# One attention and feed-forward program on one core: value windows loaded on 128 partitions, and its line of 2036 steps written anew

## The chip, the cores and the metric

The program runs on one core of one Trainium2 chip. The core has a matrix engine (PE, with its weight loads PEld), VectorE (DVE), ScalarE (ACT), GpSimd (POOL), and SyncE (SP), which here only issues DMAs. GpSimd issues DMAs too, those that add to what lies in DRAM. The metric is the device time of one execution in microseconds, lower is better. It was measured three times: 592.06 us is the median, 590.71 and 593.77 the ends.

## What is computed

Attention with a sliding window of 16 and with 24 block summaries of keys and values, then two feed-forward layers, the first with a softplus, all in fp32 accuracy:

```python
B, H, S, D = 2, 8, 768, 64;  block, window, nb = 32, 16, 24
k_sum = k.reshape(B, H, nb, block, D).max(axis=3)
v_sum = v.reshape(B, H, nb, block, D).mean(axis=3)
scores_l = where(|i - j| < window, q @ k.T / 8, -1e9)
scores_s = q @ k_sum.T / 8 + log(block)
a = softmax(concat([scores_l, scores_s]))
attn = a @ concat([v, v_sum])              # -> x: 1536 x 512
h = x @ w_in;  g = softplus(h);  x2 = g @ w_out      # 512 -> 2048 -> 512
out = ((x2 @ w1) * (x2 @ w2)) @ w3 @ w_out2          # 512 -> 1024 -> 1024 -> 512
```

## The kernel before

**Tiling.** The 12 query tiles (two batches of six) hold 128 positions each, as two blocks of 64. A block sees a window of W = 96 keys and values and the NBK = 24 summaries of its batch, together NK = 120 rows. For a tile t the steps are: `q{t}` and `vw{t}` load its queries and its two value windows; `kw{t}` and `ks{t}` copy its keys and key maxima together; `A{t}` is the score matmul; `max{t}{e}` on DVE and `exp{t}{e}` on ACT are the softmax in eight pieces; `inv`, `norm` scale; `T{t}{h}` transposes on PE, `at{t}{h}` copies that out of PSUM; `AV{t}` multiplies by the values; `xh{t}` and `xl{t}` split the result in a high and a low part, since each fp32 product is made of three passes over such parts (function `mm3`).

**Values.** `vw_load` (L372) issues one DMA for a tile: 96 partitions, on each two rows of 512 floats (2 KB), the two windows of the tile; 384 KB. The summaries come into rows 96 to 119 later: `vss{t}` sums the windows on PE, `vsT` copies the sums, and for tiles 0 and 1 they reach the value tile over PE and a copy (`vsu0`, `vs0_0`, `vs0_1`, `vs1_0`, `vs1_1`), for the others over DRAM (`vsd`, then `vs{t}`). Keys are loaded by `kp0_0` to `kp1_1` (four parts of 384 KB, batch 0) and `kl2`, `kl3` (768 KB each, batch 1); `km2`, `km3` reduce the latter on DVE.

**Feed-forward.** Weights arrive as raw fp32 (`lw...`, three raw slots called st), are made into parts by four conversions (`ca`, `cb`, `cc`, `cd`) and two splits (`ce`, `c`), on ACT, DVE and POOL. `H`, `X`, `Ph` are PE steps of the first layer (plain and, for four pairs, a seven-product scheme with sums `R`, `T` and copies `u1`, `U2`, `U3`), `sa`, `sb`, `sc`, `hi`, `lo` its softplus and split. A finished group of four goes out by `Xo` (a copy) and `Xs` (a DMA that writes, or from GpSimd one that adds to the rows in DRAM); `Xl` loads the sums back. `wm` multiplies w3 by the last weight matrix, ahead of time; `AB`, `Pp`, `O` are the second layer; `Oo` copies the output out of PSUM and `Os` stores it.

**Order.** Nothing is scheduled when it is built: the string `LINE` (L79) names all 2036 steps in the order in which they are issued, with `@` the buffer slots that a step takes and with `:A`, `:D`, `:G` the engine (ACT, DVE, POOL) where a step has a choice. `Order.order` checks that every step stands behind what it needs. Each engine works its own instructions strictly in that order and waits where an input or a slot isn't ready. The times in the code (`COST`, `PACE`, `lead`, `tail`) take no part in what is built.

```python
nc.sync.dma_start(vw[t][0:W], bass.AP(
    tensor=src.tensor, offset=src.offset, ap=[[D, W], [(w1_ - w0) * D, 2], [1, D]]))
```

Of the kernel before, what the change touches and what calls it, by code (L numbers as in the profile page):

```python
# [83 lines left out]
max16 exp25 max17 vss3 exp17 inv2 exp16 norm20:D exp15 T00@0 norm21:D inv1 T01@1 km2 at00:A@1 norm10:G vss6@1 norm11:G T10@0 vss4 at10:A@2 vss5
at01:A@3 T21@0 vsT0 km3 vsd0 vsu0@3 at21:A@4 T20@1 vs0_1:A T11@0 vs0_0:D vs1_1:A vss7 ccw_in0:D@0 at11:A@5 AV0@0 caw_in0:D cbw_in0 cdw_in0 xh0:A@1
vw8@0 vs1_0:D cew_in0:A@0 lw_in1@0 A3@1,2 xl0 caw_in3:A cw_in0:G at20:D@0 A4@0,3 q9@0 max30@0 vs5 kw6:G@2 max31 exp30 vs2 max32 AV1@0 exp31 q6@1 max33
exp32 kw7:G@0 vs3 max34 exp33 max35 vs4 max36 exp35 vw11@3 vss8 max37 exp36 max40@2 A5@1,2 exp37 max41 exp34 max42 max43 xh1:A inv3 kw8:G@1 q7@2 exp41
norm30:D exp40 exp42 norm31:G exp43 max44 ccw_in1:A@1 T30@0 xl1 exp44 max45 ks7 exp45 max46 AV2@0 max47 exp46 at30:D@1 exp47 ks6 ks8 inv4 max50@1
norm41:G max51 exp50 T31@1 exp51 vw9@2 xh2:D A6@0,3 norm40:G at31:A@3 xl2 max52 AV3@0 kw9:G@2 q8@1 max53 exp52 max54 exp53 max55 exp54 max56 T40@0
exp55 vw10@1 max57 ks9 exp56 T41@1 caw_in1:D exp57 cbw_in1 A7@1,2 at40:A@2 inv5 at41:A@5 cdw_in1 vss9 xh3:A norm50:G q10@2 max60@0 cew_in1:A@1  # L90
lw_out3@0 xl3 exp60 max61 cw_in1:G AV4@0 max62 exp61 max63 exp62 max64 exp63 max65 vss10 norm51:G exp64 max66 vss11 exp65 max67 max70@2 T50@0 kw11:G@0
max71 vsT1 exp67 vsd1 max72 T51@1 exp66 at50:D@0 xh4:A@2 A8@0,3 inv6 at51:A@4 max73 norm61:G max74 exp73 vs6 AV5@1 max75 exp74 max80@1 vs7 exp75 max81
vs10 norm60:G xl4 exp70 vs8 T61@0 xh5:A vs9 caw_in2:D kw10:G@1 q11@1 T60@1 at61:A@1 xl5 vs11 at60:A@3 ccw_in2:D@2 exp72 max76 AV6@0 max77 exp76
cbw_in2 exp77 exp71 cdw_in2 H0_0_0@1 exp81 inv7 H0_0_1 cew_in2:A@2 lw_out0@1 max82 norm70:G max83 exp82 A9@1,2 max84 exp83 max85 exp84 norm71:G max86
T70@0 exp85 max87 ks10 exp87 H0_0_2 cw_in2:G exp86 at70:D@2 xh6:A H0_0_3 cbw_in3 exp80 T71@1 He0_0:A@0 A10@0,3 inv8 at71:A@5 xl6 ccw_in3:A@3 norm81:G
H0_1_0@1 max90@0 caw_out0:A max91 AV7@0 norm80:G max92 exp90 max93 exp92 max94 cdw_in3 exp94 T80@0 xh7:A ks11 H0_1_1 max95 lw_out1@2 exp93 xl7
cew_in3:A@3 H0_1_2 max96 exp95 max97 cw_in3:G H0_1_3 at80:D@0 exp96 exp97 max100@2 T81@1 ccw_out3:D@4 He0_1:A A11@1,2 at81:A@4 max101 max102 exp91
max103 AV8@0 exp101 inv9 exp103 max104 caw_out3:D norm90:G exp104 max105 H0_2_0@1 xh8:A@0 max106 max107 exp106 H0_2_1 xl8 norm91:G exp107 H0_2_2
cbw_out3 exp105 exp102 H0_2_3 exp100 max110@1 T90@0 max111 He0_2:A@1 inv10 max112 T91@1 exp111 norm101:G max113 exp112 H0_3_0@0 max114 cdw_out3 exp113
norm100:G exp114 H0_3_1 at91:A@3 max115 H0_3_2 lw_out2@0 cbw_out0 exp115 at90:A@1 H0_3_3 cew_out3:A@2 AV9@0 max116 exp110 cw_out3:D exp116 max117  # L100
He0_3:A ccw_out0:D@0 T100@1 exp117 cdw_out0 T101@0 xh9:A at100:D@2 H1_0_0@1 lw_in4@1 at101:A@5 inv11 H1_0_1 cew_out0:A@3 caw_out1:D norm110:G xl9
caw_out2:A AV10@3 ccw_out2:D@1 spl norm111:G cbw_out1 T110@1 xh10:D H1_0_2 at110:A@0 xl10 H1_0_3 caw_in4:A cw_out0:G cbw_out2 T111@0 He1_0:A@4
H1_1_0@0 at111:A@4 H1_1_1 sa0_0@1 sa0_1@3 sb0_0 AV11@1 cdw_out2 sb0_1 sc0_0 lw_in6@0 cew_out2:A@5 H1_2@1 sc0_1 xh11:A cw_out2:G sa0_2@2 xl11 sb0_2
# [1154 lines left out]
```

## Time and profile before

| | us |
|---|---|
| median of three timed runs (lowest, highest) | 592.06 (590.71, 593.77) |
| the profiled execution | 593.24 |
| its span, first to last instruction | 591.5 |
| PE busy in the span | 551.9 |
| DVE busy | 460.5 |
| ACT busy | 274.9 |
| POOL busy | 170.2 |

The profiled execution is one run; 1.7 us of its time lie outside the span. The granted clock of PE is at its full level over most of the span and at half of it in a few stretches, 0.972 in the mean. The views used below are the page itself, the list of who waits for whom, the chain of waits that ended last, stretches of time with the busy time of each engine, the timeline, and the DMA view. SPq is SyncE issuing DMAs. A number in square brackets in a timeline row is how long the engine sat idle before the row, and what ended that.

### The profile page before, as it was taken

Reading aid. Unit: us, or ns where it says so; the run is one execution under the profiler, and the core shown is the slowest. Engines: PE = TensorE matmul, PEld = TensorE weight load, DVE = VectorE, ACT = ScalarE, POOL = GpSimd, SP = SyncE. Lnnn points to the kernel's source line nnn. Section 1 sums busy time; section 2 is a strip of 40 time slices with the busy share of each in tenths; the row PEclk is TensorE's granted clock in tenths of the full one; section 3 lists DMA queues with packets and bytes.
Section 4 is the critical chain, followed back from the end, with each engine's and each line's share of the span. In section 5 each row is a group of like instructions: output and inputs, shape, how many; then the busy total and the mean of one; then the engine's idle time right before and its main releaser. Section 6 shows DMA issues by size and latency. Waiting matters only on the chain.

```text
span 591.5 us, 8926 instructions
## 1 busy us (share of the span) xinstructions
PE 551.9 (93%) x3228; PEld 449.3 (76%) x3228; DVE 460.5 (78%) x891; ACT 274.9 (46%) x600; POOL 170.2 (29%) x152
## 2 busy tenths in 40 slices
...
GB/s 217 237 299 205 104 76 101 204 148 158 256 173 237 91 156 81 105 165 169 103 108 93 207 272 303 353 135 205 160 127 19 0 73 1 1 1 0 1 32 111
DMA packets 33621, 81.08 MB, mean 137 GB/s; under 512 B 3977, under 2 KB 4425, under 8 KB 33577
## 3 DMA queue, kind: packets, MB, share of 16 engines
...
HBM read 58.91 MB, written 21.59 MB: 136 GB/s over the span
## 4 chain that ended last, share of the span: by engine, by line
PE 48%; DVE 24%; DMA 16%; issue 5%; ACT 4%; POOL 1%; SPq 1%; DVEq 0%; ACTq 0%; POOLq 0%
PE abps L711 17%; PE ops L223 11%; PE abps L223 7%; DMA raw<-in_w_dram 6%; PE wps L223 4%; PE xps L223 3%; DVE cv L266 3%; DVE raw L254 3%; DMA kt<-in_k_dram 3%; PE hps L223 2%; DVE gt L232 2%; DMA qt<-in_q_dram 2%; DVE tm L500 2%; DMA x_d<-xo 2%; DVE cv L262 2%
## 5 line engine op out<-in xcount | busy, mean ns | idle before, releaser
L223 PE MATMUL xps<-gt,w 128*128 128x512 f32 x576 | 136.3, 389 | 0.0
L223 PEld LDWEIGHTS xps<-gt,w 128*128 128x128 f32 x576 | 108.1, 188 | 22.5
L223 PE MATMUL hps<-xt,w 128*128 128x512 f32 x384 | 93.9, 393 | 3.5 <-DVE gt L232 3.5
L232 POOL TENSOR_TENSOR w<-cv,w 128x512 fp32r<-128x512 f32 x34 | 50.7, 1497 | 137.0 <-ACT w L227 89.7
L223 PEld LDWEIGHTS hps<-xt,w 128*128 128x128 f32 x384 | 71.1, 188 | 19.4 <-DVE gt L232 4.8
L223 PE MATMUL ops<-w,pt 128*128 128x512 f32 x288 | 70.3, 389 | 0.0
L254 DVE SCALAR_TENSOR_TENSOR raw<-raw 128x512 int32<-128x512 int32 x72 | 57.0, 796 | 9.5 <-ACT raw L250 9.2
L223 PEld LDWEIGHTS ops<-w,pt 128*128 128x128 f32 x288 | 54.1, 188 | 11.2
L266 DVE SCALAR_TENSOR_TENSOR cv<-cv,raw 128x512 int32<-128x512 int32 x72 | 55.4, 779 | 1.3
L532 POOL DMA_DIRECT2D x_d<-xo x36 | 32.6, 1079 | 79.1 <-ACT xo L227 72.7
L250 ACT ACTIVATE raw<-raw 128x512 int32<-128x512 uint16 x53 | 35.7, 674 | 35.8 <-DMA raw<-in_w_dram 19.4
L723 DVE TENSOR_TENSOR u<-u,abps 128x512 f32<-128x512 f32 x36 | 24.6, 684 | 34.0 <-PE abps L711 20.1
L223 PE MATMUL wps<-w 128*128 128x512 f32 x192 | 47.0, 407 | 3.3 <-DVE w L229 3.3
L503 ACT ACTIVATE tm<-tm 128x512 f32<-128x512 f32 x48 | 29.7, 631 | 41.7 <-DVE tm L500 37.8
L223 PEld LDWEIGHTS wps<-w 128*128 128x128 f32 x192 | 37.9, 198 | 12.1 <-ACT w34o L227 3.7
L227 ACT CAST w<-cv 128x512 fp32r<-128x512 f32 x59 | 35.6, 619 | 22.7 <-DVE cv L266 10.3
L223 PE MATMUL abps<-x2t,w 128*128 128x512 f32 x192 | 44.5, 389 | 0.0
L415 ACT ACTIVATE s<-s,sm 128x120 f32<-128x120 f32 x96 | 36.8, 386 | 10.8 <-DVE sm L409 10.7
L223 PEld LDWEIGHTS abps<-x2t,w 128*128 128x128 f32 x192 | 36.0, 188 | 7.5
L260 ACT ACTIVATE cv<-raw 128x512 f32<-128x512 f32 x48 | 31.7, 671 | 14.9 <-DMA raw<-in_w_dram 7.9
L711 PE MATMUL abps<-t,s 128*128 128x512 f32 x144 | 36.5, 390 | 0.0
L227 ACT COPY u<-abps 128x512 f32<-128x512 f32 x26 | 14.9, 587 | 44.8 <-PE abps L711 33.3
(128 smaller groups left out, 878.9 us busy)
## 6 DMA issues: line engine op xcount, KB each, us to landing
...
```

The lines of the kernel that those rows point to most:

```text
L223: nc.tensor.matmul(ps, lhs(a), rhs(b), start=first and i == 0, stop=last and i == 2)
L227: nc.scalar.copy(d, s_)
L232: EN[eng].tensor_tensor(d, a, b, ALU.subtract)
L250: nc.scalar.activation(r[:, :, 0], r.bitcast(U16)[:, :, 1], AF.Copy, bias=-(0.5 - 2.0 ** -14), scale=2.0 ** -13)
L254: nc.vector.scalar_tensor_tensor(r[:, :, 0], r[:, :, 1], -0x80000000, r[:, :, 0], ALU.bitwise_and, ALU.bitwise_or)
L260: nc.scalar.activation(f(c), h, AF.Copy, scale=2.0 ** -112)
L266: nc.vector.scalar_tensor_tensor(c, c, 3, r[:, :, 0], ALU.logical_shift_left, ALU.bitwise_or)
L415: nc.scalar.activation(s[:, e], s[:, e], AF.Exp, bias=sm[:, 0, e:e + 1], scale=-1.0, accum_out=sm[:, 1, e:e + 1])
L503: nc.scalar.activation(tm[c, i], tm[c, i], AF.Softplus)
L532: nc.gpsimd.dma_start(x2_d[4 * c + o], xo[c, g, o], accum_op=ALU.add)
L711: nc.tensor.matmul(ps, w[:, a, (o + kk) * P:(o + kk + 1) * P], rhs(b), start=k in (1, 5, 2) and kk == 0 and n == 0, stop=kk == 1 and n == ...
L723: nc.vector.tensor_tensor(tu[z, j, d], tu[z, j, d], bank[z, j, k], ALU.add)
```

## The change

Two things change: the value load, and the line.

```diff
@@ vw_load
-                four[0] = xt_p.tile([NK, 4, 2, D], F32, tag=slot("xt"), name="vw4")
+                four[0] = xt_p.tile([P, 4, 2, D], F32, tag=slot("xt"), name="vw4")
...
-            vw[t] = ap_.tile([NK, 2, D], F32, tag=slot("vw"), name="vw")
-        nc.sync.dma_start(vw[t][0:W], bass.AP(
-            tensor=src.tensor, offset=src.offset, ap=[[D, W], [(w1_ - w0) * D, 2], [1, D]]))
+            vw[t] = ap_.tile([P, 2, D], F32, tag=slot("vw"), name="vw")
+        n = P if w1_ + P <= S else W
+        nc.sync.dma_start(vw[t][0:n], bass.AP(
+            tensor=src.tensor, offset=src.offset, ap=[[D, n], [(w1_ - w0) * D, 2], [1, D]]))
@@ att_d1
-                        vw[t][:, blk, 64 * h:64 * h + 64],
+                        vw[t][:NK, blk, 64 * h:64 * h + 64],
@@ LINE, its first and its last row
-sz ml kp0_0@0 z@0 sell1 busy@0 sell0 sell2 kp0_1 kp1_0@1 kp1_1 q0@0 vw0@0 vw3@1 q1@1 vw2@2 kn0_0 q2@2 vw4@0 vw5 vw1@3 vw6 kw0:A@0 kw1:D@1 il kl2@2
...
-O20_0 O21_0 O23_2 O22_0 O23_0 Oo20:D@5 Oo22:A@2 Oo23:D@0 Os20 Os22 Oo10:D@4 Os23 Oo21:D@1 Os10 Os21
...
+Oo20:A@2 O17_3 Os20 O18_3 O23_2 O17_1 O18_1 O19_1 O20_1 O21_1 O22_1 O23_1 O19_3 Oo21:A@3 O20_3 Oo10:A@0 Oo12:D@5 Os21 Oo11:A@4 Os10 O21_3 Oo22:A@1
+Os12 O22_3 Oo13:A@2 Os11 Os22 O23_3 Os13 Oo23:D@3 Os23
```

The load now fills 128 partitions (512 KB) for ten of the tiles; for tiles 5 and 11 the second window ends at the last row of the input, and they stay at 96. Rows 96 to 119 are still overwritten by the summaries, rows 120 to 127 are read by nobody. The line holds the same 2036 steps in another order, with other slots, and 252 of them on another engine; PE has the same 3228 matmuls. Steps other than DMAs on POOL are 104 (99 before), and 76 (70 before) of them stand ahead of the first `AB`; DVE instructions are 896 (891).

Three places, as the built programs have them. A row is a source line (one more after the change), the operation, what is written and read, and its size.

SP at the start of the program; `vw` and `vw4` are value tiles, `kt` keys, `qt` queries, `sel_t` a small constant. Before:

```order
L303 DMA kt_172<-in_k_dram 128x768 x2
L364 DMA qt_175<-in_q_dram 128x512
L381 DMA vw_177<-in_v_dram 96x2x512
L381 DMA vw_179<-in_v_dram 96x2x512
L364 DMA qt_181<-in_q_dram 128x512
L381 DMA vw_183<-in_v_dram 96x2x512
L364 DMA qt_187<-in_q_dram 128x512
L381 DMA vw4_189<-in_v_dram 96x2x512 x2
L381 DMA vw_192<-in_v_dram 96x2x512
L381 DMA vw4_189<-in_v_dram 96x2x512
L897 DMA id_t_127<-in_ident_dram 128x128
L303 DMA kt_202<-in_k_dram 128x1536
```

After:

```order
L303 DMA kt_170<-in_k_dram 128x768 x2
L382 DMA vw_173<-in_v_dram 128x2x512
L332 DMA sel_t_128<-in_sel_dram 64x2
L364 DMA qt_176<-in_q_dram 128x512
L364 DMA qt_178<-in_q_dram 128x512
L382 DMA vw_180<-in_v_dram 128x2x512
L898 DMA id_t_127<-in_ident_dram 128x128
L364 DMA qt_183<-in_q_dram 128x512
L382 DMA vw4_185<-in_v_dram 128x2x512
L382 DMA vw4_185<-in_v_dram 96x2x512
L382 DMA vw4_185<-in_v_dram 128x2x512
L332 DMA sel_t_128<-in_sel_dram 64x2
```

The same loads stand between the fourth key part and the large key loads; all but one are wider, and their order among themselves is another.

ACT in the middle of the first layer; `u_2944` before and `u_2937` after is the copy `U3h5`, `raw_2879` before is the raw weight tile w3 6 (`caw36` works on it), `raw_2769` after is w_out 12. Before:

```order
L227 CAST gt_2913<-hps_2861 128x512
L250 ACTIVATE raw_2874<-raw_2874 128x512
L260 ACTIVATE cv_2923<-raw_2874 128x512
L250 ACTIVATE raw_2879<-raw_2879 128x512
L227 COPY u_2944<-abps_2622 128x512
L227 CAST w_2947<-cv_2882 128x512
```

After:

```order
L260 ACTIVATE cv_2907<-raw_2859 128x512
L227 CAST gt_2911<-u_2713 128x512
L260 ACTIVATE cv_2920<-raw_2769 128x512
L227 COPY u_2937<-abps_2616 128x512
L227 CAST w_2944<-cv_2920 128x512
L504 ACTIVATE tm_2955<-tm_2955 128x512
```

`caw36` is no longer ahead of the copy (it went to DVE); the conversion ahead of it now reads a tile whose load is issued 13 PE steps earlier.

SP where the sums of the first layer are loaded back (`x2f`, steps `Xl0_0` to `Xl0_3`); `raw_3557` before and `raw_3281` after is the raw weight tile w3 8 (step `lw38`). Before:

```order
L539 DMA x2f_3408<-x2_d2_111 128x512
L539 DMA x2f_3400<-x2_d1_110 128x512
L539 DMA x2f_3408<-x2_d3_112 128x512
L273 DMA cv_3459<-pk_wo23_88 128x512
L273 DMA cv_3472<-pk_w35_98 128x512
L273 DMA cv_3477<-pk_wo24_89 128x512
L269 DMA pk_wo27_92<-cv_3497 128x512
L241 DMA raw_3520<-in_w3_dram 128x1024
L273 DMA cv_3527<-pk_wo25_90 128x512
L273 DMA cv_3534<-pk_w36_99 128x512
L269 DMA pk_wo26_91<-cv_3525 128x512
L241 DMA raw_3557<-in_w3_dram 128x1024
```

After:

```order
L241 DMA raw_3198<-in_w3_dram 128x1024
L273 DMA cv_3209<-pk_w30_93 128x512
L241 DMA raw_3226<-in_wo2_dram 128x1024
L273 DMA cv_3271<-pk_w31_94 128x512
L269 DMA pk_wo26_91<-cv_3260 128x512
L241 DMA raw_3281<-in_w3_dram 128x1024
L273 DMA cv_3289<-pk_wo20_85 128x512
L540 DMA x2f_3424<-x2_d0_109 128x512
L540 DMA x2f_3424<-x2_d1_110 128x512
```

The load of w3 8 and the store `pkwo26` (`pk_wo26`) stood behind the loads of the sums and now stand ahead of them.

## Rows read from the trace of the kernel before

**Rows 1.** The page, part 1: busy time of PE, share, instructions.
```profile
PE 551.9 (93%) x3228; PEld 449.3 (76%) x3228; DVE 460.5 (78%) x891; ACT 274.9 (46%) x600; POOL 170.2 (29%) x152
```

**Rows 2.** Stretches: length, busy us (instructions) by engine, PE clock, DMA share, GB/s.
```profile
11.60:37.30 25.70, 15.14 (x256) 11.86 (x256) 14.15 (x69) 12.49 (x54) 6.05 (x9) 0.73 1.05 273
37.30:93.00 55.70, 49.99 (x844) 41.08 (x844) 49.60 (x216) 51.10 (x187) 30.78 (x36) 0.97 0.50 139
...
400.00:585.00 185.00, 184.86 (x816) 152.75 (x814) 131.17 (x196) 53.17 (x90) 41.12 (x29) 1.00 0.15 50
```

**Rows 3.** The chain of waits at 19 to 35 us, at 261 and 351: start, us, what.
```profile
19.26 15.50 DMA kt<-in_k_dram
34.79 1.75 DVE ks L308
...
260.82 9.80 DMA raw<-in_w_dram
...
351.42 17.76 DMA raw<-in_w_dram
```

**Rows 4.** Timeline: the last key part's reduction on DVE, and `AV0` on PE.
```profile
10.26 0.95 DVE L308 TENSOR_REDUCE ks<-kt 128x24 f32<-128x768 f32 x1 [0.99 <-DMA kt<-in_k_dram]
...
37.33 0.86 PE L453 MATMUL av<-at,vw 120*64 120x64 f32 x22 [1.93 <-DVE vw L229]
```

**Rows 5.** DMA view of 10 to 22 us, of 32 to 36, of 586.4 to 589.9.
```profile
DMA packets 1458, 2.75 MB, mean 229 GB/s; under 512 B 124, under 2 KB 124, under 8 KB 1457
...
DMA packets 475, 1.57 MB, mean 393 GB/s; under 512 B 54, under 2 KB 54, under 8 KB 474
...
DMA packets 707, 1.30 MB, mean 373 GB/s; under 512 B 70, under 2 KB 70, under 8 KB 707
```

**Rows 6.** The page, part 5: groups, with busy us and mean ns of one.
```profile
L254 DVE SCALAR_TENSOR_TENSOR raw<-raw 128x512 int32<-128x512 int32 x72 | 57.0, 796 | 9.5 <-ACT raw L250 9.2
...
L415 ACT ACTIVATE s<-s,sm 128x120 f32<-128x120 f32 x96 | 36.8, 386 | 10.8 <-DVE sm L409 10.7
```

**Rows 7.** Timeline: a DVE step held by POOL at 142.
```profile
142.52 1.78 DVE L254 SCALAR_TENSOR_TENSOR raw<-raw 128x512 int32<-128x512 int32 x1
```

**Rows 8.** Timeline around 231 us: `ccwo24` on DVE, `R11` and `cw_in13` on POOL, `Ph2_4`.
```profile
231.34 4.55 DVE L262 TENSOR_SCALAR cv<-raw 128x512 f32<-128x512 f32 x1
...
234.03 1.56 POOL L232 TENSOR_TENSOR w<-cv,w 128x512 fp32r<-128x512 f32 x1
235.81 0.68 DVE L254 SCALAR_TENSOR_TENSOR raw<-raw 128x512 int32<-128x512 int32 x1
...
237.15 2.49 PE L711 MATMUL abps<-xt,w 128*128 128x512 f32 x6 [3.64 <-DVE gt L232]
```

**Rows 9.** Timeline around 271 us: `caw36` and `U3h5` on ACT, `Ph4_5` on PE.
```profile
270.71 0.65 ACT L250 ACTIVATE raw<-raw 128x512 int32<-128x512 uint16 x1 [0.97 <-DMA raw<-in_w_dram]
271.26 0.56 ACT L227 COPY u<-abps 128x512 f32<-128x512 f32 x1
...
271.88 2.50 PE L711 MATMUL abps<-t,w 128*128 128x512 f32 x5 [2.90 <-ACT u L227]
```

**Rows 10.** Timeline: the issue of `lw38` on SP, and `wm8` on PE.
```profile
342.67 0.42 SPq L241 DMA_DIRECT2D raw<-in_w_dram  x1
...
375.01 7.19 PE L223 MATMUL wps<-w 128*128 128x512 f32 x18 [3.27 <-DVE w L229]
```

**Rows 11.** Stretches behind the first and last of those waits, columns as in rows 2.
```profile
237.70:241.10 3.40, 3.40 (x9) 2.67 (x8) 1.12 (x1) 1.43 (x3) 0.67 (x1) 0.50 0.71 236
...
374.20:381.00 6.80, 5.99 (x14) 4.72 (x15) 6.40 (x13) 6.80 (x13) 0.00 (x0) 0.50 1.03 374
```

**Rows 12.** Timeline of the last 12 us: the last `O` steps, `Oo` copies, `Os` stores.
```profile
579.72 5.15 PE L223 MATMUL ops<-w,pt 128*128 128x512 f32 x22
...
584.90 2.48 DVE L229 COPY osb<-ops 128x512 f32<-128x512 f32 x4 [10.27 <-PE ops L223]
585.62 2.41 SPq L746 DMA_DIRECT2D out_dram<-osb  x5
```

More of the change, by code (lines that the diff above doesn't have):

```diff
@@ L84 @@
[L84 to L103, printed above, removed]
@@ L128 @@
-sa0_9@0 ccw35:A@3 lo0_8 sb0_9 X2_5_1 caw35:A sc0_9 R10:G@6 cbw35 hi0_9:A@5 H0_10@1 cew_out11:A@4 ccw_in14:A@4 caw_in14:A cw_out11:G Th1s Ph1_4@1 cdw35
-Th1h:A@0 X2_6_0 sa0_10@3 pkw35 lwo24@1 u1h4:A@0 Th1l sb0_10 X2_6_1 sc0_10 X2_7_0 R21:G@0 hi0_10:D@2 lo0_10 X2_7_1 lo0_9 cawo24:A cbw_in14 H0_11@1 Th3s
-Th2s Th3h:A Ph5_4@0 Th3l Th2h:A@1 Ph1_5@0 Th2l sa0_11@5 Xo21_2:A@4 Ph6_4 Xo21_3:A@1 cdw_in14 Xs21_2 sb0_11 Xo21_0:D@2 Xs21_3 lwo25@2 X0_8_1@0,3
-U2h4:A@1 sc0_11 Xs21_0 u1h5:A@2 ccwo24:D@0 hi0_11:A@1 R11:G@6 cbwo24 Ph6_5 Xo21_1:A@0 lo0_11 cew_in14:A@4 cdwo24 cew_in13:A@1 Ph2_4@1 Ph7_4 cw_in13:G
@@ L136 @@
-pkw32 lw36@0 lo1_9 ccw_out15:A@2 caw_out15:D X1_9_1 Xo02_2:A@0 sa0_12@3 upwo20@3 sa1_10@4 Xs02_2 sb0_12 cbw_out15 X1_8_0@3,0 sb1_10 sc0_12 sc1_10
-hi0_12:A@6 X1_9_0 caw_out12:A lo0_12 ccw_out12:A@4 hi1_10:D@4 cbw_out12 H0_13@0 lo1_10:D caw36:A cdw_out15 U3h5:A@2 cdw_out12 cew_out15:A@0 lw_out13@1
-C22h5 cew_out12:A@3 lw_out14@2 cw_out15:G Ph4_5 cbw36 cw_out12:G Ph3_5 sa1_11@5 sa0_13@1 sb1_11 X1_10_0 C12h5 Shh71:A@2 sb0_13 sc1_11 Slh71:G H0_14@1
-sc0_13 caw_out14:A hi1_11:D@5 hi0_13:D@2 lo1_11 lo0_13 X1_10_1 sa0_14@2 cbw_out14 sb0_14 H0_15@0 ccw36:D@2 upw30@4 sc0_14 upwo21@0 caw_out13:D
@@ L156 @@
-cew37:A@3 cdw38 caw310:A cbw315 cew312:A@5 Xl1_3 lw311@1 cw312:D Xl1_1 wm6 cw37:G ccw310:A@0 cbw310 ccw39:A@4 cdw310 wm3 Xl2_2@3 cdw39 Xl2_0@5 lw20@2
-cew39:A@0 lw10@0 cw39:D wm7 cew38:D@1 wo0:A@0 cw38:D wo1:A@1 ws0 caw311:A ccw311:D@1 ws1 ccw314:A@4 cbw311 Xl2_3 x2h10:A@2 cdw314 wm8@0,1 Xl2_1
-wo3:D@3 wo2:A@2 cdw311 cew314:A@2 ws3 ws2 caw20:A cw314:D lw21@1 cew313:A@0 cbw20 ccw10:A@2 wm9 cw313:D ccw20:A@4 cew310:D@1 caw10:A cdw20 cw310:G
-x2h11:A cbw10 lw11@2 cdw10 cew20:A@1 wm12@0,1 cew311:A@0 x2h21:A@0 cw311:G cw20:D lw12@0 x2l21 wm10 caw21:D ccw21:A@3 caw11:A cew10:D@4 cbw21 cw10:G
@@ L184 @@
-Ph23:D@3 Pl23:D O15_1 O15_0 O15_2 O18_0 Oo12:D@4 O15_3 Os12 O18_2 Oo11:D@3 Oo13:A@1 O19_2 Os13 Os11 O21_3 O20_2 O23_1 O22_3 O21_2 O22_2 O23_3 O19_0
-O20_0 O21_0 O23_2 O22_0 O23_0 Oo20:D@5 Oo22:A@2 Oo23:D@0 Os20 Os22 Oo10:D@4 Os23 Oo21:D@1 Os10 Os21
+sz ml z@0 kp1_0@0 kp1_1 busy@0 sell1 kp0_0@1 kp0_1 vw2@0 sell0 q0@0 q1@1 vw0@1 il q2@2 vw4@0 kn0_0 vw5 vw6 sell2 kn0_1 kw0:A@0 vw1@2 kw1:A@1 kw2:G@2
+vw3@3 kn1_0 kl2@2 vw7 kn1_1 kl3@3 lw_in1@0 ks0 lw_in0@1 ks1 A0@1,2 ks2 lw_in3@2 A1@3,0 max00@0 kw4:G@0 q3@0 max01 exp00 max02 exp01 max03 exp02 max04
@@ new lines @@
+exp03 max05 max06 exp05 kw5:G@1 q5@1 max10@1 exp06 max11 exp04 max12 exp10 max13 max07 exp12 A2@1,3 max14 max15 exp07 max16 exp15 inv0 exp13 q4@2
+norm01:D vss0@0 norm00:G exp14 exp11 ks4 ks5 max20@2 exp16 max21 exp20 vss1 max22 exp21 max23 kw3:G@2 exp22 max24 T00@0 max17 exp24 max25 exp17 ks3
+max26 exp23 inv1 vss2 exp26 max27 norm11:G at00:A@1 vss3 exp27 km2 exp25 norm10:G vss4 vss5 inv2 norm20:D T01@1 norm21:G vsT0 vsd0 vsu0@2 at01:A@2 km3
+T11@0 vs1_1:A T10@1 vs0_1:A vs0_0:D ccw_in1:A@0 vs1_0:D AV0@1 caw_in0:A ccw_in0:D@1 at11:A@3 at10:D@4 vss6@0 xh0:A@1 vw8@1 cbw_in0 vss7 caw_in3:A xl0
@@ new lines @@
+Xo11_0:A@1 Xs11_2 hi2_6:A@1 Xo11_3:D@3 R21:G@2 ccw_in14:A@4 lo2_6 Xo11_1:D@4 X2_4_1@2,3 cew_in13:A@0 sa2_7@0 cdw_in14 sb2_7 cw_in13:G X2_4_0@1,0
+Xs11_0 H0_8@0 cew_out10:A@3 Xs11_3 sc2_7 lw35@2 cw_out10:G hi2_7:D@3 lo2_7 Xs11_1 ccw_out11:A@3 cdw31 X2_5_1 sa0_8@5 pkw31 lwo24@0 cdw_out11 sb0_8
+H0_9@1 Ss1h6 lw_in15@1 sc0_8 Ss3h6 hi0_8:A@4 R10:G@6 Ss2h6 X2_6_1 caw35:A R20:G@5 X2_7_1 ccw35:A@1 Ph1_4@1 Th1s X2_5_0 u1h4:A@0 cawo24:A sa0_9@2
+Th1h:A@0 X2_6_0 lo0_8 Th3s sb0_9 H0_10@0 cew_out11:A@1 sc0_9 Th1l hi0_9:A@0 lo0_9 X2_7_0 Th2s Th3h:D H0_11@1 Th2h:A@1 Th3l Xo21_1:A@0 Xs21_1 Th2l
@@ new lines @@
+Ph1_5@0 sa0_10@1 sa0_11@5 sb0_10 Ph6_4 Xo21_0:D@3 sb0_11 sc0_10 Xo21_2:A@4 Xs21_0 sc0_11 X0_8_0@0,1 hi0_10:A@1 Xs21_2 U2h4:A@1 Ss4h6 lo0_10 hi0_11:A@6
+R11:G@3 Ph7_4 lo0_11 cw_out11:D Ph5_4@0 U3h4:A@2 Th4s Ph2_4@1 Shh60:A@0 Slh60:G C22h4 Th4h:A@2 X0_9_0 C11h4 cew_in14:A@2 Th4l Ph3_4 cw_in14:G
+Xo21_3:A@1 sa1_8@2 u1h5:D@3 sb1_8 Ph4_4 C12h4 sc1_8 Xs21_3 Ph6_5 cbw35 hi1_8:A@5 ccw_in15:D@3 ccwo24:A@0 lo1_8:D X0_8_1@2,3 cdw35 U2h5:A@0 caw_in15:D
+pkw35 Ph2_5@1 cbw_in15 lw_out13@2 cdw_in15 X0_10_0 lw_out12@1 C11h5 upwo21@1 cew_in15:D@3 cbwo24 Ph7_5 cdwo24 cw_in15:D pkwo24 X0_9_1 caw_out13:A
@@ new lines @@
+lw_out14@0 Ss1h7 Ss3h7 Ph5_5@0 cbw_out13 Ss2h7 Ss4h7 X0_10_1 Shh61:A@2 Shh71:D@1 Slh71:D Slh61:D X0_11_0 caw_out14:A ccw_out14:D@0 caw_out12:D
+cbw_out14 X0_11_1 Xo02_1:A@5 sa1_9@0 Xs02_1 cdw_out14 sb1_9 H0_12@1 Xo02_2:A@3 sc1_9 lwo25@0 Xs02_2 cew_out14:D@2 hi1_9:A@2 cbw_out12 cw_out14:G lo1_9
+X1_8_1@1,2 sa0_12@4 Xo02_0:D@2 Xo02_3:A@1 sb0_12 X1_9_1 sa1_10@0 Xs02_0 sb1_10 sc0_12 Xs02_3 sc1_10 hi0_12:A@3 X1_8_0@3,0 ccwo25:A@3 cawo25:D lo0_12
+hi1_10:A@4 X1_9_0 cbwo25 ccw_out12:A@2 lo1_10:G cdwo25 H0_13@1 U3h5:A@3 cdw_out12 pkwo25 lw36@0 C22h5 cew_out12:A@0 lw32@1 cw_out12:G Ph4_5 sa0_13@5
```

157 lines of the change are left out of this document (86 added, 71 removed).

## The prediction

> **What bounds the kernel now.** I read the page's part 1 first [rows 1]: PE is busy 551.9 of 591.5 us. So the question is where PE is not working, or works at half its clock. The stretches answer it [rows 2]. From 400 to 585 us PE is busy 184.86 of 185: no order of its instructions gains there, since the change leaves PE its 3228 matmuls. In the first stretch, 11.6 to 37.3 us, PE has 15.14 us of work in 25.7 us; this is the head. Between 37.3 and 93 us PE (49.99), DVE (49.60) and ACT (51.10) are all nearly full in 55.7 us, so nothing catches up a late head there, and a head that ends earlier should carry through. The timeline then shows three waits of PE of about 3 us each in the middle, at 237, 272 and 375 us [rows 8 to 10], and behind them stretches at half clock [rows 11]. Last, the tail: the last matmuls end at 579.72 + 5.15 = 584.87 us and the span ends at 591.5, 6.6 us later [rows 12].
>
> **The value loads and the head.** The chain of waits has the large key loads until 34.79 us, then their reduction (1.75 us) [rows 3], and two copies later the first value product `AV0` starts at 37.33 [rows 4]. These loads queue behind the value loads. The last of the four first key parts is in at 10.26 us [rows 4]. Between that and 34.79 the queue moves, by the sizes of the rows of the order, three query loads (0.786 MB), eight value loads of 0.393 (3.146), the identity (0.066) and two key loads (1.573): 5.57 MB in 24.5 us, 227 GB/s. The rates are uneven: 229 GB/s at 10 to 22 us, where mostly value loads on 96 partitions move, and 393 at 32 to 36, where a 128-partition key load moves [rows 5]. The same 2 KB packets, on all partitions, go out 1.7 times as fast.
>
> After the change seven of the eight carry 0.524 MB, so the queue has 6.49 MB. At 393 GB/s that is 16.5 us, 8.0 less than now. At the mean of the whole first stretch, 273 GB/s [rows 2], it is 23.8 us, 0.7 less. I take 8.0, since a load on 128 partitions is what the 393 was measured on, and keep 0.7 as the other end. ACT could become the bound of the head: about 24 `exp` steps at 0.386 us [rows 6] and five copies at 0.56 (the size of the one in [rows 9]) stand ahead of the first products, 12.1 us, from about 12.7 us (the last key part is reduced at 10.26 + 0.95 = 11.2 [rows 4], and a key copy and the score product follow, taken as 1.5): 24.8 us, before the new `AV0` at 37.33 − 8.0 = 29.3. So ACT doesn't hold it.
>
> [...]
>
> **The three waits.** *Site A*, `Ph2_4`: PE waits 3.64 us. `ccwo24` sits on DVE for 4.55 us from 231.34, while POOL works off `R11` and then `cw_in13` until 235.6; the next DVE step takes 0.68 [rows 8]. After, `ccwo24` is on ACT and `cw_in13` is earlier, but `R11` remains, with other DVE steps beside it. *Site B*, `Ph4_5`: 2.90 us. The copy `U3h5` stands on ACT behind `caw36` [rows 9], whose weights were 9.80 us on the way from 260.82 [rows 3]; after, `caw36` is on DVE, and the conversion ahead of the copy reads a load that is issued 13 PE steps earlier. *Site C*, `wm8`: 3.27 us. `lw38` was issued at 342.67 [rows 10], and `cw38` stands on DVE behind the conversion of w3 10, which came 17.76 us after 351.42 [rows 3]; after, `lw38` is ahead of the loads of the sums, and `cw38` is ahead of `wm6` and of the conversion of w3 10. Behind A PE runs 3.40 us at a clock of 0.50, behind C 6.80 us [rows 11]; half of that is lost, 1.7 and 3.4; for B I take A's 1.7. Gross: (3.64 + 1.7) + (2.90 + 1.7) + (3.27 + 3.4) = 16.6 us.
>
> What is late next? A line that was written anew in all its places will have waits of its own that no row of before can show. The lower end is that all 16.6 stays won, the upper that waits as large come up elsewhere and nothing is won. I take B and C as gone (4.6 + 6.7), A as half gone (2.7), together 14.0, less new waits of the size of one site, 16.6 / 3 = 5.5: 8.5 won.
>
> **POOL.** A DVE step beside POOL work can be held: the split L254 took 1.78 us at 142 us [rows 7] against 0.68 unheld [rows 8], 1.10 more. Its mean over 72 is 796 ns [rows 6], so (0.796 − 0.68) × 72 / 1.10, some 8 of 72, are held. Six more POOL steps ahead of the second layer hold none (0) or one DVE step each (6.6). DVE is near its limit up to 93 us only, so I take 1.5 lost.
>
> **The tail.** Before, after PE's last matmul DVE makes four output copies (2.48 us), and five stores are issued from 585.62 on [rows 12]; their data move until about 589.9 at 373 GB/s, 0.70 us for 0.262 MB [rows 5], and the span ends 1.6 us later. After, only `Oo23` and its store are left behind the last PE step; the copies of the other tiles stand one PE step or more ahead, so their stores are under way. The new line still ends with seven stores: some twelve matmuls stand behind the first one's issue, at 5.15 / 22 = 0.23 us each [rows 12] 2.7 us, and from an issue to its data pass 0.8 (585.62 to 586.4), so data move from 1.9 us before PE ends; 7 × 0.70 = 4.9 puts the last byte at +3.0, the end at +4.6 instead of +6.6: 2.0 won, ends 1 (the last copy, 0.62, and its own issue and landing stay whatever is ahead) and 3.
>
> **The sum.** Against the profiled execution, 593.24: − 8.0 (head) − 8.5 (waits) − 2.0 (tail) + 1.5 (POOL) = 576.2. The profiled run lies 1.2 above the median of 592.06, so the forecast is **575.0 us**.
>
> **Rivals.** Each is worked out as this sum with one term put to its end.
> *All three waits go, and no new ones come*: 16.6 instead of 8.5, 567.0. For it: each of the three has its own cause, removed in the order. Against it: DVE and ACT are loaded throughout, and a step brought forward pushes others back.
> *New waits as large as the old*: 0 instead of 8.5, 583.5. For it: `R11` stays on POOL and DVE steps stand beside it; all 2036 steps moved.
> *The queue gains nothing*: 0.7 instead of 8.0, 582.3. For it: bytes go up by 0.92 MB, and the rate of 10 to 22 us might come from something other than the partitions, such as many small query loads beside them. Against it: the 229 and the 393 of [rows 5] are of equal packets. [...] With the rival before it as well, 593.24 − 0.7 − 2.0 + 1.5 − 1.2 = 590.8, no change.
> *Slower*: the POOL steps hold DVE as at 231 us. There one hold cost PE 3.64 us and 1.7 of clock, 5.3 [rows 8, 11]. With the waits at 583.5, three more such places make 599.5, and from the third on the kernel is slower than before by more than 0.5%. For it: six more POOL steps, and DVE steps of all engines' chains beside them. Against it: one place of this size in the whole trace of before, with 70 such steps.
>
> **Chances.** The forecast, its terms off by their smaller parts (about 570 to 580), 0.37; all waits gone 0.18; new waits as large 0.20; no gain in the queue 0.13; both of the last two 0.06; slower 0.06. From 565 to 588 the range holds all but the last two and what lies below 565. Half a per cent, 3 us, is what a measurement of this kernel can tell from no change: 589.1 to 595.0 is the same. Faster 0.88, same 0.06, slower 0.06.
>
> **What would show it.** In the profile after: `AV0` at 29 to 30 us, and the DMA view of 10 to 22 us near 390 GB/s; if it shows 230 to 270 and `AV0` is past 36, the head's term was wrong. At 93 us's place in the work (the start of the second group of the first layer) the lead of 8 must still be there; if not, ACT or DVE ate it. `Ph4_5` and `wm8` start without a wait over 1 us; between there and the second layer the waits over 2 us and the stretches at half clock sum to some 5 us. No DVE step of 4 us beside POOL. From the last matmul to the end 4.6 us. Anything that holds PE in the second layer, which is full now, would make all of it wrong.

## The result, and the profile after

The changed kernel takes 570.97 us (median of four runs, 569.54 to 572.24) against 592.91 for the kernel before (four runs): a ratio of 0.9623, 95% interval 0.9568 to 0.9678, so 19 to 26 us less. The forecast was 575.0, with 565 to 588 as its range. The profiled execution took 571.06, its span 569.3, which stands against the 593.24 and 591.5 before.

The page of the changed kernel, busy times and the group of L254 (before: [rows 1, 6]):

```profile
PE 548.0 (96%) x3228; PEld 445.2 (78%) x3228; DVE 468.2 (82%) x896; ACT 267.6 (47%) x587; POOL 171.9 (30%) x160
...
L254 DVE SCALAR_TENSOR_TENSOR raw<-raw 128x512 int32<-128x512 int32 x72 | 51.4, 719 | 1.3 <-ACT raw L250 0.9
```

To see where the 22.2 us of span went, both are cut at the same three places of the work: the start of `AV0`, the end of `AV11` (the last product of the attention), and the end of PE's last matmul. Columns as in [rows 2]. Before:

```profile
0.00:37.33 37.33, 23.33 (x285) 15.02 (x285) 18.78 (x77) 14.73 (x58) 7.01 (x15) 0.82 0.96 255
37.33:94.14 56.81, 51.13 (x875) 42.15 (x875) 50.72 (x218) 52.11 (x189) 30.78 (x36) 0.97 0.49 136
94.14:584.86 490.72, 477.40 (x2070) 392.14 (x2070) 388.54 (x594) 208.04 (x355) 132.43 (x101) 0.99 0.45 127
584.86:591.50 6.64, 0.00 (x1) 0.00 (x0) 2.48 (x4) 0.00 (x0) 0.00 (x0) 0.83 0.53 197
```

After:

```profile
0.00:30.75 30.75, 20.22 (x244) 13.03 (x245) 17.07 (x70) 15.43 (x59) 9.78 (x20) 0.89 0.97 334
30.75:86.07 55.32, 52.31 (x906) 41.75 (x906) 49.31 (x218) 49.60 (x184) 29.89 (x37) 0.97 0.46 149
86.07:564.78 478.71, 475.41 (x2079) 390.38 (x2079) 401.17 (x610) 202.59 (x344) 132.20 (x103) 1.00 0.46 131
564.78:569.30 4.52, 0.00 (x1) 0.00 (x0) 0.69 (x1) 0.00 (x0) 0.00 (x0) 0.87 0.65 244
```

Up to the end of `AV11` 8.1 us are gone (94.14 to 86.07), from there to the last matmul 12.0 (490.72 to 478.71), in the tail 2.1 (6.64 to 4.52). Some PE work has moved from the first part to the second, so I also count by waits: PE's idle time, plus half of the time in which it is busy at half clock, summed from the trace's matmuls and clock records. (Half is an estimate: at a clock of 0.50 PE took 0.38 and 0.43 us a matmul, 9 in 3.40 and 14 in 5.99 [rows 11], against 0.23, 22 in 5.15 [rows 12].) Up to `AV11` that falls from 25.1 to 18.3 us (−6.8), in the middle from 13.3 + 6.4 = 19.7 to 3.3 + 1.7 = 5.0 (−14.7), in the tail −2.1; the work itself, at full clock, reads 1.4 more. The sum is −22.2.

**The head.** DVE's last key reduction (`km3`) and the two value copies, and `AV0` on PE, after (before: [rows 3, 4]):

```profile
28.21 1.75 DVE L308 TENSOR_REDUCE ks<-kt 128x48 f32<-128x1536 f32 x1 [0.45 <-DMA kt<-in_k_dram]
30.00 1.31 DVE L229 COPY vw<-vs_p 24x512 f32<-24x512 f32 x2
...
30.75 1.15 PE L454 MATMUL av<-at,vw 120*64 120x64 f32 x32 [1.75 <-DVE vw L229]
```

The DMA view of 10 to 22 us, after (229 GB/s before [rows 5]):

```profile
DMA packets 2101, 4.05 MB, mean 338 GB/s; under 512 B 229, under 2 KB 357, under 8 KB 2100
```

The key load is in at 28.2 instead of 34.8 us, and `AV0` follows it 2.54 us later, as it did before (34.79 to 37.33). It still waits 1.75 us, for a copy (`vs0_0`) that stands on DVE behind `km3`, which `AV0` doesn't need.

**Site A again.** The timeline around 221 us, after: DVE's L682 is `Ss4h6`, POOL's L627 is `R11`, PE's row is `Ph5_4`.

```profile
221.28 3.64 DVE L682 TENSOR_TENSOR cv<-cv 128x256 f32<-128x256 f32 x1
...
221.64 2.99 POOL L627 TENSOR_TENSOR xf<-xt 128x1024 f32<-128x1024 f32 x1
...
225.58 0.73 PE L712 MATMUL abps<-t,s 128*128 128x512 f32 x2 [1.98 <-DVE gt L232]
```

and the stretch behind it:

```profile
226.70:230.20 3.50, 3.50 (x10) 2.77 (x9) 1.85 (x4) 1.67 (x3) 1.29 (x1) 0.51 0.00 0
```

This is the mechanism of [rows 8] with another DVE step in it. It is the only wait over 0.7 us that PE has behind 35 us. `Ph4_5` and `wm8` (inside the second row) start without one:

```profile
258.73 1.52 PE L712 MATMUL abps<-t,w 128*128 128x512 f32 x6
...
351.76 12.40 PE L223 MATMUL wps<-w 128*128 128x512 f32 x54
```

The step of site A is not the longest that DVE has beside POOL. At 199 us one of L266, else 0.68, takes 6.00 us beside two POOL steps, and PE goes on without a wait:

```profile
199.36 6.00 DVE L266 SCALAR_TENSOR_TENSOR cv<-cv,raw 128x512 int32<-128x512 int32 x1
...
199.77 5.03 POOL L627 TENSOR_TENSOR xf<-xt 128x1024 f32<-128x1024 f32 x2
...
203.67 2.88 PE L223 MATMUL xps<-gt,w 128*128 128x512 f32 x12
```

**The tail**, after (before: [rows 12]); PE ends at 564.78:

```profile
561.42 2.55 ACT L227 COPY osb<-ops 128x512 f32<-128x512 f32 x5 [6.89 <-PE ops L223]
...
562.03 3.89 SPq L747 DMA_DIRECT2D out_dram<-osb  x7
564.88 0.69 DVE L229 COPY osb<-ops 128x512 f32<-128x512 f32 x1 [10.92 <-PE ops L223]
```

One copy is left after the last matmul, and seven stores are issued from 2.8 us before it on.

### The profile page after: what moved, and what is told of

Its sections match the earlier page's. It is cut to its first block, busy times and chain, and to the rows that moved or that the text cites. A ratio compares the mean times of both kernels' runs of the same rounds, so it can differ in the third digit from the quotient of the medians.

```text
span 569.3 us, 8940 instructions
## 1 busy us (share of the span) xinstructions
PE 548.0 (96%) x3228; PEld 445.2 (78%) x3228; DVE 468.2 (82%) x896; ACT 267.6 (47%) x587; POOL 171.9 (30%) x160
## 4 chain that ended last, share of the span: by engine, by line
PE 75%; DVE 8%; DMA 7%; ACT 5%; issue 2%; POOL 1%; SPq 1%; POOLq 0%; DVEq 0%; ACTq 0%
PE abps L712 19%; PE xps L223 16%; PE hps L223 12%; PE ops L223 11%; PE abps L223 8%; PE wps L223 6%; DMA kt<-in_k_dram 3%; ACT s L416 2%; DMA vw<-in_v_dram 1%; DVE cv L266 1%; DMA raw<-in_w_dram 1%; PE av L454 1%; PE tr L436 1%; DVE w L232 1%; DVE cv L682 1%
## 5 line engine op out<-in xcount | busy, mean ns | idle before, releaser
L223 PE MATMUL xps<-gt,w 128*128 128x512 f32 x576 | 138.7, 390 | 0.7 <-DVE xo L229 0.7
L232 POOL TENSOR_TENSOR w<-cv,w 128x512 fp32r<-128x512 f32 x35 | 52.8, 1514 | 122.5 <-ACT w L227 107.9
L266 DVE SCALAR_TENSOR_TENSOR cv<-cv,raw 128x512 int32<-128x512 int32 x72 | 56.7, 798 | 1.3
L254 DVE SCALAR_TENSOR_TENSOR raw<-raw 128x512 int32<-128x512 int32 x72 | 51.4, 719 | 1.3 <-ACT raw L250 0.9
L223 PE MATMUL wps<-w 128*128 128x512 f32 x192 | 44.5, 390 | 0.3 <-DVE w L232 0.3
L223 PEld LDWEIGHTS wps<-w 128*128 128x128 f32 x192 | 36.0, 188 | 8.2 <-DVE w L232 0.7
L260 ACT ACTIVATE cv<-raw 128x512 f32<-128x512 f32 x42 | 27.7, 671 | 12.9 <-DVE w L232 4.5
L712 PEld LDWEIGHTS abps<-t,s 128*128 128x128 f32 x144 | 26.9, 188 | 8.1 <-DVE gt L232 2.4
```

The lines of the kernel that those rows point to most:

```text
L223: nc.tensor.matmul(ps, lhs(a), rhs(b), start=first and i == 0, stop=last and i == 2)
L232: EN[eng].tensor_tensor(d, a, b, ALU.subtract)
L254: nc.vector.scalar_tensor_tensor(r[:, :, 0], r[:, :, 1], -0x80000000, r[:, :, 0], ALU.bitwise_and, ALU.bitwise_or)
L260: nc.scalar.activation(f(c), h, AF.Copy, scale=2.0 ** -112)
L266: nc.vector.scalar_tensor_tensor(c, c, 3, r[:, :, 0], ALU.logical_shift_left, ALU.bitwise_or)
L712: nc.tensor.matmul(ps, w[:, a, (o + kk) * P:(o + kk + 1) * P], rhs(b), start=k in (1, 5, 2) and kk == 0 and n == 0, stop=kk == 1 and n == ...
```

## The experiments

Names of steps are those of the line. A line that is moved is shown with its neighbours.

**The wide loads alone, on the old line** (`old_wide`): the two hunks of the change at `vw_load` and `att_d1`, the line left as before.

```diff
-        nc.sync.dma_start(vw[t][0:W], bass.AP(
+        n = P if w1_ + P <= S else W
+        nc.sync.dma_start(vw[t][0:n], bass.AP(
```

> The kernel before with one part of the change alone: ten value loads on 128 partitions, the line of steps untouched. Theory, partitions set the speed of these loads (about 150 ns per 2 KB packet on 96 partitions, 84 to 88 ns on 128): from 10 to 22 us the DMA view shows 350 to 400 GB/s instead of 229, the third large key load is in at 28 to 29 us instead of 34.8, and AV0 starts at 30 to 31.5 us instead of 37.3. In time 5 to 7 us less than the kernel before if the lead carries through, since DVE and ACT are nearly full up to 93 us. [...]

Ratio to the kernel before 0.9933 (0.9898 to 0.9969): 4.0 us less, 1.8 to 6.0. `AV0` starts at 32.06, the last key load is in at 29.26. Its DMA view of 10 to 22 us:

```profile
DMA packets 2186, 4.16 MB, mean 347 GB/s; under 512 B 156, under 2 KB 239, under 8 KB 2185
```

The rate, 347 GB/s against 229 [rows 5], is the doing of the loads' partitions (and of the bytes that come with them): nothing else was changed. All four figures fall a little short of what was expected: 347 of 350 GB/s, the key load 0.3 us later, `AV0` 0.6 later, 4.0 us gained instead of 5 to 7.

**The changed kernel with narrow loads** (`new_narrow`).

```diff
-        n = P if w1_ + P <= S else W
+        n = W
```

> The changed kernel with all value loads on 96 partitions again, its line untouched. Theory, partitions set the speed: AV0 back at 36 to 38 us instead of 30.75, and 5 to 7 us more than the changed kernel (about 577). Rival, the order of the loads made the gain: AV0 within 1 us of 30.75, time within 2 us of the changed kernel.

Ratio to the kernel before 0.9708 (0.9667 to 0.9749), where the changed kernel has 0.9623 in its own runs and 0.9649 beside `new_best` below: the wide loads are worth some 3.5 to 5 us here. These runs are of different chips, and the intervals of 0.9708 and 0.9649 overlap a little, so the size is rough. `AV0` is at 32.24, not back at 36 to 38:

```profile
32.24 1.81 PE L454 MATMUL av<-at,vw 120*64 120x64 f32 x32 [3.14 <-DVE vw L229]
```

So both theories missed on `AV0`: with the same bytes per load as before, the new order alone has it 5.1 us earlier than in [rows 4]. Up to 3.2 of these 5.1 can be a difference between executions, as the next kernel shows.

**Four hand edits to the old line** (`old_fixed`), narrow loads: each one mends a cause that the prediction named, all in one kernel.

```diff
-hi0_11:A@1 R11:G@6 cbwo24 ... ccwo25:A@3 Th4s
+hi0_11:A@1 cbwo24 ... ccwo25:A@3 R11:D@6 Th4s
-caw36:A cdw_out15 U3h5:A@2
+cdw_out15 U3h5:A@2 caw36:A
-caw310:A cbw315 cew312:A@5 ... wm3 ... wm7 cew38:D@1 wo0:A@0 cw38:D wo1:A@1
+caw310:A cbw315 wm3 cew38:D@1 cw38:D wo0:A@0 wo1:A@1 cew312:A@5 ... wm7
-O23_1 ... O23_3 ... O23_2 O22_0 O23_0 Oo20:D@5 Oo22:A@2 Oo23:D@0 Os20 Os22 Oo10:D@4 Os23 Oo21:D@1 Os10 Os21
+Oo10:D@4 Os10 ... O23_1 Oo21:D@1 Os21 ... O23_3 Oo23:D@0 Os23 ... O23_2 Oo22:A@2 Os22 O22_0 O23_0 Oo20:D@5 Os20
```

> The kernel before with four hand edits to its line, each for one stated cause: R11 from POOL to DVE, behind the copies that PE waits for; U3h5 ahead of caw36 on ACT; cew38 and cw38 on DVE and the copies wo0 and wo1 on ACT ahead of the conversions of w3 12 and w3 10; each output copy right behind its own last product instead of four behind the last one. Theory, the waits have these causes and nothing comes back: the waits of Ph2_4 (3.64), Ph4_5 (2.90) and wm8 (3.27) fall below 0.7 each, the three stretches at half clock behind them go, and the tail falls from 6.6 to 4.6: 9.8 less at most 1.5, and 6.8 of clock, and 2.0, so 16 to 18 us less (about 575 against 592). Rival, the waits move on: new waits of PE over 1 us between 230 and 400 us that are not in the kernel before, and a gain under 9 us, the tail included. Rival for the tail: stores are what ends it, and it stays at 6 to 6.6.

Ratio 0.9797 (0.9744 to 0.9849): 12.0 us less (9.0 to 15.2), not 16 to 18. PE's timeline has `Ph2_4`, `Ph4_5` and `wm8` (inside the third row) without a wait, and what is late next:

```profile
236.76 1.53 PE L711 MATMUL abps<-xt,w 128*128 128x512 f32 x6
...
267.44 1.59 PE L711 MATMUL abps<-t,w 128*128 128x512 f32 x6
...
359.76 14.52 PE L223 MATMUL wps<-w 128*128 128x512 f32 x63
374.89 10.72 PE L223 MATMUL wps<-w 128*128 128x512 f32 x46 [0.61 <-POOL w L232]
385.94 0.73 PE L223 MATMUL wps<-w 128*128 128x512 f32 x2 [0.33 <-ACT w L227]
387.57 2.56 PE L223 MATMUL wps<-w 128*128 128x512 f32 x10 [0.90 <-DVE w L232]
```

The same cuts as above, from `AV11` to the last matmul, and the tail:

```profile
96.51:575.12 478.61, 472.08 (x2071) 387.49 (x2070) 389.23 (x598) 208.52 (x355) 130.23 (x100) 1.00 0.47 132
575.12:579.00 3.88, 0.00 (x0) 0.00 (x0) 0.69 (x1) 0.00 (x0) 0.00 (x0) 1.00 0.36 135
```

Here 490.72 has become 478.61, at full clock throughout, and the tail 3.88: in the parts that were edited 14.9 us are gone. New waits are 0.42 (at 244 us) and 1.84 (the `wm` rows), so the three causes are shown, each at its own place; the waits that came in their place are small. What is missing in the profile's total lies ahead of 96.51 us, where nothing was edited: `AV11` ends 2.4 us later than before, though `AV0` starts 3.2 earlier. By the count of waits PE is idle 2.7 us less there and loses 5.0 more to half clock, as the row of the first 70 us shows (0.88 in the kernel before, last section):

```profile
0.00:70.00 70.00, 53.01 (x836) 39.34 (x837) 45.29 (x210) 43.58 (x173) 27.05 (x41) 0.80 0.80 223
```

and the key reduction and `AV0`, on the very loads of the kernel before:

```profile
31.58 1.75 DVE L308 TENSOR_REDUCE ks<-kt 128x48 f32<-128x1536 f32 x1 [1.64 <-DMA kt<-in_k_dram]
...
34.12 1.87 PE L453 MATMUL av<-at,vw 120*64 120x64 f32 x32 [1.53 <-DVE vw L229]
```

The same queue took until 34.79 in [rows 3] and until 31.58 here. So two executions of the same instructions differ by 3.2 us at this place, and [rows 3, 4] show the later one. Of the 6.6 us by which `AV0` is earlier in the profile of the changed kernel, up to 3.2 can be this spread. Measured from 34.12, the wide loads alone (32.06) bring it 2.1 us forward, the new order alone (32.24) 1.9, both (30.75) 3.4, each read from one profile.

**Loads and hand edits together** (`old_all`): `old_fixed` with the wide loads.

> The kernel before with the wide value loads and the four hand edits of old_fixed together. If the gains add up: 4 (old_wide) + 12 (old_fixed) = 16 less than the kernel before, 0.973, so 5 to 6 above the changed kernel; what is then left of the change is in the order elsewhere (waits of H at 160, 192 and 214 us, 1.3 to 1.5 each, and the wm steps). Rival: the gains overlap, and it stays within 2 us of old_fixed.

577.65 us, 0.9749 (0.9712 to 0.9786): the two gains add up, 15 us, nearly the 16 expected. The changed kernel, measured beside it on one chip (`after_again` below), is 5.7 us below that. Their profiles differ by 4.8: by the same cuts 4.1 ahead of the end of `AV11` (90.34 here, 86.23 there) and 1.3 in the middle, less 0.6 in the tail, which is shorter here. Of the 4.1 the count of waits gives 0.1 to PE's idle time, 2.9 to half clock and 1.1 to work that the new line does later.

**The changed kernel once more** (`after_again`), nothing edited.

> The changed kernel as it is, beside the others of this set on one chip, since half-clock stretches of PE in the first 70 us came out differently in each profile so far (3.4 us of them in one, 27 in another). Expected 0.960 to 0.965 of the kernel before. If the stretches before 70 us belong to the execution and not to the kernel, this profile shows others than the 11.7, 22.0 and 32.2 us of the first one, and the values of AV0 differ by 1 us or more.

571.91 us, 0.9649 (0.9609 to 0.9689). The half-clock stretches of this profile lie within 0.1 us where they lay in the first one, and `AV0` is at 30.66 (30.75). So in this kernel they came out the same in two executions, which those of the kernel before and `old_fixed` did not.

**Two steps moved in the changed kernel** (`new_both`).

```diff
-at01:A@2 km3 T11@0 vs1_1:A T10@1 vs0_1:A vs0_0:D ccw_in1:A@0 vs1_0:D AV0@1
+at01:A@2 T11@0 vs1_1:A T10@1 vs0_1:A vs0_0:D ccw_in1:A@0 vs1_0:D km3 AV0@1
-hi0_11:A@6 R11:G@3 Ph7_4 lo0_11 cw_out11:D Ph5_4@0
+hi0_11:A@6 Ph7_4 lo0_11 cw_out11:D R11:D@3 Ph5_4@0
```

> The changed kernel with two steps moved: the reduction km3 on DVE behind the copies vs0_0 and vs1_0 that AV0 needs (before, vs0_0 waits for km3, AV0 waits 1.75 us), and R11 from POOL to DVE behind lo0_11 and cw_out11 (Ss4h6 was held for 3.64 us beside R11, Ph5_4 waits 1.98 and PE then runs 3.4 us at half clock). Theory: AV0 at 29.0 to 29.3, Ph5_4 without a wait over 0.3 us and no half clock behind it, so 1.7 + 2.0 + 1.7 = 5.4 us less than the changed kernel at most (565 to 566.5). Rival: DVE has no room, so km3's and R11's time (1.75 and 1.1 us) come back as waits of A6 or of later products, and the gain is under 2 us.

567.86 us, 0.9589 (0.9551 to 0.9627): by the ratios 2 to 3.6 us less than the changed kernel, where 5.4 was the most expected and under 2 the rival. `AV0` starts at 28.19, 2.6 earlier, `AV11` ends 1.5 earlier. DVE and PE around the old site A (L682 `Ss4h6`, the PE row `Ph5_4`):

```profile
219.78 0.42 DVE L682 TENSOR_TENSOR cv<-cv 128x256 f32<-128x256 f32 x1
...
221.94 1.55 PE L712 MATMUL abps<-t,s 128*128 128x512 f32 x6
```

`Ss4h6` takes 0.42 us instead of 3.64 without `R11` beside it; the wait and the half clock behind it are gone. That shows POOL's step as the cause of the hold.

**Three steps more** (`new_best`): `q3` ahead of `lw_in1`, `vs0_1` ahead of `vs1_1`, `at20` ahead of `xl1`.

> The changed kernel with km3 behind the two value copies and R11 on DVE, as in new_both, and three steps more: the query load q3 ahead of the three weight loads lw_in1, lw_in0, lw_in3 (A3 waited 1.70 us for it once AV0 was early), vs0_1 ahead of vs1_1 on ACT (vs0_0 waited 0.37 for it), at20 ahead of xl1 on DVE (AV2 waited 1.39). Theory: AV0 at 27.7, A3 without a wait, AV2's wait 0.4 less: 1.5 to 2.5 less than new_both, 565 to 566.5, 0.953 to 0.957 of the kernel before. Rival: the attention is held by ACT and DVE anyway and the time is that of new_both within 1 us.

567.73 us, 0.9581 (0.9542 to 0.9621): that of `new_both`, so the rival held. In the profile `AV0` is at 30.41, not 27.7, and PE runs at a clock of 0.50 from 13.6 to 27.2 us, so this profile doesn't tell what the three steps are worth. Beside `after_again` on one chip its six runs (567.05 to 568.99) lie below all six of the changed kernel (570.48 to 574.94): 4.2 us, 0.7%.

**What slows a load on 96 partitions?** The changed kernel with 112 (`new_112`), and with 64 and 32 as two loads (`new_64_32`).

```diff
-        n = P if w1_ + P <= S else W
+        n = 112 if w1_ + P <= S else W
```

> The changed kernel with ten value loads on 112 partitions. It asks what slows a load on 96. [...] If a load that doesn't fill 128 partitions is cut up in another way, its packets take 140 to 155 ns at 112 too and the DMA view of 10 to 22 us shows 230 to 290 GB/s. If the slowing goes by share, packets take 100 to 120 ns, 290 to 340 GB/s.

The DMA view of 10 to 22 us:

```profile
DMA packets 1739, 2.95 MB, mean 246 GB/s; under 512 B 211, under 2 KB 339, under 8 KB 1738
```

The 2 KB packets of 12 to 22 us take 136 to 152 ns in the median of each 2 us. 112 partitions go at no higher rate than 96, 246 GB/s against 253 (`new_narrow`), with more bytes: `AV0` is at 35.26, 3 us later than with 96, and the one run took 579.18 us.

```diff
-            nc.sync.dma_start(vw[t][0:n], ... ap=[[D, n], ...
+        for a, b in ((0, 64), (64, W)):
+            nc.sync.dma_start(vw[t][a:b], ... offset=src.offset + a * D, ap=[[D, b - a], ...
```

> The changed kernel with each value load as two DMAs, partitions 0 to 63 and 64 to 95, so 96 in all. It asks whether it is the cut of one load over the DMA engines that slows it or the partitions that it reaches. [...]

```profile
DMA packets 1815, 2.90 MB, mean 241 GB/s; under 512 B 316, under 2 KB 444, under 8 KB 1814
```

As slow again: with the same 96 partitions in two loads the view shows 241 GB/s, in one 253 (`new_narrow`), so this cut brings no gain; `AV0` is at 33.56, the one run took 575.83. With loads of 64 and 32, of 96 and of 112 partitions the view shows 229 to 253 GB/s, with loads of 128 332 to 348 where one narrow load is among them.

**The load that stayed narrow** (`best_t5`): `new_best` with tile 5 at 128 as well.

```diff
-        n = P if w1_ + P <= S else W
+        n = P if w1_ + P <= S or t == 5 else W
```

> new_best with the value load of tile 5 on 128 partitions too: its second window reads 32 rows into the next batch, which nobody uses. In all profiles of wide loads so far the rate falls to 209 to 279 GB/s for about 4 us at 14 to 18 us, where that load on 96 partitions is in the queue. Theory: no such dip is left before 22 us (every stretch of 2 us at 350 or more), the large key loads land 0.5 to 1.5 us earlier, and the time is 0 to 1.5 us below new_best (566 to 567.7), too little for an interval to tell. Rival: the dip is due to the other loads at that place (queries, small ones) and stays.

```profile
DMA packets 2352, 4.66 MB, mean 388 GB/s; under 512 B 242, under 2 KB 370, under 8 KB 2351
```

The dip is gone: 388 GB/s over 10 to 22 us, where `new_best` has 342. So value loads that are all wide do move at nearly the 393 of [rows 5]. In time, 567.35 (0.9575, 0.9514 to 0.9637), it can't be told from `new_best`.

## Why the prediction was right, and where it was off

The time fell where the prediction said, and within its range, though 4 us lower than the likeliest case. That it came so close is in part luck: two of its terms were off by 4 us and more, in opposite ways.

- **The head, −8.0.** The mechanism is right: with the load size alone changed, the rate rises from 229 to 347 GB/s. The size is too large: the loads by themselves give 4.0 us on the old line and some 3.5 to 5 on the new one. That the profiles show 8.1 up to `AV11` is no proof of the term, since the new order and the spread between executions are in it. What went wrong in the term: the 24.5 us of queue came from one execution, and the same queue took 3.2 us less in `old_fixed`. The trace has more in these 24.5 us than the 5.57 MB summed up from the order, because weight loads that were issued later are under way before the last key load is in (DMA view of 10.26 to 34.79 us):

```profile
DMA packets 2610, 6.35 MB, mean 259 GB/s; under 512 B 237, under 2 KB 365, under 8 KB 2606
```

  The 393 of [rows 5] isn't of equal packets either: 1.57 MB in 475 packets is 3.3 KB in the mean. And one load of the eight stayed narrow (338 in the mean). The rate that it took was nearly right all the same (388 in `best_t5`). That `AV0` follows the queue was right, 2.5 to 3.1 us behind its end in all nine profiles with `km3` in its place, but only DVE's order ties it there: with `km3` moved (`new_both`) it starts at 28.19, ahead of that reduction. That ACT wouldn't hold the head was right. The lead carried through: 6.6 at `AV0`, 8.1 at the end of `AV11`, of which 1.2 is PE work that the new line does later; in `old_fixed` a lead of 3.2 was lost to the clock.
- **What slows the narrow loads.** That loads on 128 partitions go at a higher rate than loads on 96 or 112 was shown, why was not. From 0.393, 0.459 and 0.524 MB at 253 (`new_narrow`), 246 (`new_112`) and 388 GB/s (`best_t5`), times of 1.55, 1.87 and 1.35 us for one load on 96, 112 and 128 partitions can be estimated: the load with the most bytes takes the least time. In two parts, of 64 and 32, the loads of 96 go no faster (241, `new_64_32`).
- **The three waits, −8.5.** B and C went entirely. Of A's 3.64 us and 1.7 of clock 1.98 and 1.7 stayed, so 1.7 went where 2.7 was said: `R11` holds another DVE step. The term was too small, and the measured one is −14.7. The step that failed is the allowance for new waits, 5.5: all waits behind `AV11` other than site A's come to 1.3 us. The gross sum also left out three smaller waits of before, 3.5 us together, that went too. Two of them, on PE:

```profile
160.69 3.02 PE L223 MATMUL hps<-xt,w 128*128 128x512 f32 x12 [1.05 <-DVE gt L232]
...
214.07 2.11 PE L223 MATMUL hps<-xt,w 128*128 128x512 f32 x8 [1.51 <-DVE gt L232]
```

  So the rival "all three waits go, and no new ones come" was nearer in the middle, with 16.6.
- **POOL, +1.5.** No such loss shows, though no run prices the term by itself. L254's mean fell from 796 to 719 ns, so by the prediction's formula its holds cost (0.719 − 0.68) × 72 = 2.8 us instead of 8.4. But L254 is one form of many. The sign "no DVE step of 4 us beside POOL" failed, with 6.00 at 199 us, and over all DVE steps beside POOL ones the time beyond their form's median comes to some 49 us in either trace, by an estimate from their rows. What a hold costs is set by what waits for the held step: the 6.00 us cost PE nothing, `R11`'s 3.64 a wait of 1.98, and no other wait of PE behind 80 us is over 0.5 in this profile. The rival "slower" needed three such places on top of old waits.
- **The tail, −2.0.** −2.1, by the mechanism named. `old_fixed` shows it in the old line, 6.64 to 3.88.

What stays open: the 5.7 us between `old_all` and the changed kernel. In the profiles the largest part of them is half clock ahead of the end of `AV11`. Whether that belongs to the new order or to the executions no run tells.
